# An attention and channel-mixing kernel: weights scaled in plain order and read with a step, some transposes by DMA, tiles in pairs, a new order

## The chip, the cores and the metric

The kernel runs on one core of one Trainium2 chip. The metric is device time in microseconds. Each version is launched several times; one launch is recorded by the hardware profiler, and its "span" runs from the first to the last instruction. The timed figure lies some 2 us above the span (170.61 against 168.7 for the profiled run of the kernel before).

In the profile the engines are PE (TensorE matmuls), PEld (its weight loads, which run beside matmuls), DVE (VectorE), ACT (ScalarE), POOL (GpSimd) and SP (SyncE, which here only issues DMAs).

## The reference

Two parts. First a linear attention with decay: for each of 8 heads of width 48 and each of 4 batches, a 48x48 state runs over 768 steps.

```python
for t in range(S):
    cur = np.einsum('bhd,bhe->bhde', u[None] * kt, vt)
    y[:, :, t] = np.einsum('bhd,bhde->bhe', rt, state + cur)
    state = w[None, :, :, None] * state + np.einsum('bhd,bhe->bhde', kt, vt)
```

Then, on rows of 8 x 48 = 384 channels, a normalization and a channel mix:

```python
xn = (x - mu) / np.sqrt(var + 1e-06) * g_ln
ch = np.maximum(xn @ w_ch1, 0.0) @ w_ch2      # 384 -> 1536 -> 384
return x + ch
```

## The kernel before

The 3072 rows are cut into 24 tiles of 128. For each tile the kernel loads r, k and v, scales r and k by powers of w, turns both (transposes them, so that channels lie on partitions), forms the 128x128 products of r and k for each head, masks them, multiplies by v, adds the state's share, normalizes, turns the normalized row, and runs the two matmul layers: "up" (384 to 1536, with w1) and "down" (1536 to 384, with w2). The last step of a tile is its eviction `ot`, then the store.

Everything is scheduled by hand. One long string, `PLAN`, lists the steps in program order as `name,index,engine` (v is DVE, s is ACT, g is POOL); each engine executes its share of the list in that order. `TR` and `LT` are the turns by PE (of r and k, and of the normalized row), `SW` scales a piece of w1 by minus g, `UP`, `RL` and `DN` are the up matmuls, the relu and the down matmuls, `ST` the statistics, `AM` the mask, `IW2` the load of a third of w2 and `LW1` of a third of w1. `DU` gives PE empty matmuls (on the tile `warm`) while it has nothing else to do.

The parts that matter here:

```python
GROUPS = [1, 1, 1, ...]        # 24 groups of one tile
w1_sb = [[const.tile([P, FB, P], BF16, ...) for kc in range(CK)] for n in range(NW)]   # FB = 4 blocks of 128

def SW(i, e):
    n, kc = divmod(i, CK)
    o, s = w1_sb[n][kc][:].rearrange("p a q -> p q a"), w1_f[n][:, kc].rearrange("p (q a) -> p q a", a=FB)
    g = g_neg[:, kc : kc + 1]
    if e == "s":
        nc.scalar.activation(out=o, in_=s, func=ACT.Copy, scale=g)
    elif e == "v":
        nc.vector.tensor_scalar(out=o, in0=s, scalar1=g, scalar2=None, op0=ALU.mult)
    ...

def UP(i, e):
    ...
            for kc in range(CK):
                nc.tensor.matmul(
                    out=t[:, a * gw : (a + 1) * gw],
                    lhsT=w1_sb[n][kc][:, fb],
                    rhs=xT(g)[:, kc, :gw], ...)
```

`SW` gathers the 512 columns of a piece into four blocks, column 4q + a into block a. After that each block is a contiguous weight for `UP`.

## Time and profile before

| | kernel before |
|---|---|
| time, median of 3 runs | 170.84 us (170.42 to 170.99) |
| span of the profiled run | 168.7 us |
| first tile's eviction starts | 39.5 us |
| eighteenth tile's (tile 17's) eviction starts | 135.7 us |
| last eviction starts | 165.1 us |

The page's busy shares and four of its rows by slice. Each digit is the busy tenth in one fortieth of the span (4.2 us); PEclk is the clock that was granted to PE, in tenths of full speed:

```profile
PE 151.2 (90%) x2185; PEld 121.6 (72%) x2185; DVE 135.7 (80%) x280; ACT 85.7 (51%) x134; POOL 86.4 (51%) x133
PE   7998284398999999999899899999999999999991
ACT  3368999951165544355544256446542644542340
PEclk9999959999999999999999999999999999999999
DMA  5999998802999699959799898971011110110211
```

PE is busy 90% of the span, but slices 5 to 8 show 2, 8, 4 and 3: there it waits, ACT is at 9, and the clock drops once.

### The profile page before, as it was taken

To read this page: it belongs to the slowest core of one execution; us is meant where nothing else is said; L and a number is where in the kernel's file an instruction comes from. 1 tells how busy PE (TensorE), PEld (TensorE's weight loads), DVE (VectorE), ACT (ScalarE), POOL (GpSimd) and SP (SyncE) were. 2 spreads that over 40 slices of the span, in tenths; PEclk is the share of its full clock that TensorE was granted. 3 is DMA by queue.
4 is the path that set the end of the run, shared out by engine and by line. 5 is a ranking of instruction groups with operands and counts; after the bars stand their busy time and mean duration, and the time that the engine had idled before them with its cause. 6 is when DMAs were issued, how large, how long until landed. Compare 5 with 4: busy or idle time off the path is not lost.

```text
span 168.7 us, 5218 instructions
## 1 busy us (share of the span) xinstructions
PE 151.2 (90%) x2185; PEld 121.6 (72%) x2185; DVE 135.7 (80%) x280; ACT 85.7 (51%) x134; POOL 86.4 (51%) x133
## 2 busy tenths in 40 slices
PE   7998284398999999999899899999999999999991
PEld 4978183385677878787688678879786788896770
DVE  3579629078999899999999999999969999787411
ACT  3368999951165544355544256446542644542340
POOL 3547949013296457932671598635532769462200
PEclk9999959999999999999999999999999999999999
DMA  5999998802999699959799898971011110110211
GB/s 87 208 254 279 294 177 158 134 8 57 215 183 202 150 207 196 198 148 207 151 203 229 164 231 175 201 140 51 0 51 47 51 47 4 47 49 4 96 47 47
DMA packets 81225, 22.75 MB, mean 135 GB/s; under 512 B 76593, under 2 KB 79666, under 8 KB 81202
## 3 DMA queue, kind: packets, MB, share of 16 engines
q1 hardware_dynamic: 79938, 21.24, 55.2%
q0 software_dynamic: 432, 1.18, 4.1%
q8 instruction: 17, 0.28, 0.7%
q10 hardware_dynamic: 832, 0.00, 0.3%
q14 instruction: 6, 0.05, 0.1%
HBM read 18.88 MB, written 4.72 MB: 140 GB/s over the span
## 4 chain that ended last, share of the span: by engine, by line
PE 60%; DVE 18%; ACT 13%; DMA 3%; issue 2%; POOL 1%; SPq 0%; DVEq 0%
PE hp L496 21%; PE o L524 20%; ACT w_sb L313 10%; PE tr L345 4%; PE o L261 3%; DVE ot L534 3%; PE at L364 3%; DVE A L374 3%; DMA out_dram<-ot 3%; DVE q L202 2%; PE y L445 2%; PE tr L481 2%; PE y L437 1%; PE s L408 1%; DVE sck L202 1%
## 5 line engine op out<-in xcount | busy, mean ns | idle before, releaser
L496 PE MATMUL hp<-xT,w_sb 128*128 128x128 bf16 x864 | 58.1, 220 | 7.4 <-ACT w_sb L313 3.6
L512 ACT ACTIVATE hT<-hp 128x512 bf16<-128x512 f32 x69 | 42.2, 615 | 44.2 <-PE hp L496 43.0
L496 PEld LDWEIGHTS <-w_sb 128*128 128x128 bf16 x864 | 51.5, 98 | 11.1 <-ACT w_sb L313 5.9
L524 PE MATMUL o<-w_sb,hT 128*128 128x384 bf16 x288 | 56.2, 326 | 1.0 <-DVE ot L534 1.0
L427 POOL TENSOR_TENSOR Vb<-vf,cc 128x384 f32<-128x384 f32 x24 | 22.0, 916 | 29.7 <-DVE cc L199 16.0
L524 PEld LDWEIGHTS <-hT 128*128 128x128 bf16 x288 | 24.9, 97 | 13.8 <-issue 1.3
L374 DVE TENSOR_TENSOR A<-at,mask 128x1024 bf16<-128x1024 f32 (+1 forms) x26 | 29.3, 1128 | 3.1 <-PE at L364 3.0
L534 DVE SCALAR_TENSOR_TENSOR ot<-o,rs,x 128x384 f32<-128x384 f32 x24 | 14.7, 611 | 8.0 <-PE o L524 7.6
L202 POOL TENSOR_TENSOR Z<-ZS,WLZ 128x384 bf16<-128x384 f32 x16 | 17.0, 1065 | 6.9 <-DVE ZS L421 6.8
L313 ACT ACTIVATE w_sb<-w_f,g_neg 128x512 bf16<-128x512 f32 x7 | 18.1, 2660 | 0.0
L473 POOL TENSOR_SCALAR rs<-mv 128x1 f32<-128x1 f32 x24 | 6.9, 287 | 19.2 <-DVE mv L459 18.2
L476 POOL TENSOR_TENSOR rs<-rs,expo 128x1 f32<-128x1 f32 x24 | 14.5, 604 | 2.0
L452 DVE TENSOR_TENSOR x<-y,Vb 128x384 f32<-128x384 f32 x24 | 13.4, 557 | 2.1 <-POOL Vb L427 1.5
L197 ACT COPY xT<-tr 128x384 bf16<-128x384 bf16 x15 | 8.0, 535 | 13.7 <-PE tr L481 13.7
L202 DVE TENSOR_TENSOR sck<-kf,Fk 128x384 bf16<-128x384 f32 x19 | 10.9, 575 | 4.1 <-ACT Fk L278 3.6
L197 ACT COPY trs<-tr 128x1024 bf16<-128x1024 bf16 (+1 forms) x12 | 10.3, 871 | 6.7 <-PE tr L345 6.7
L455 DVE BATCH_NORM_STATS2 stats<-x 128x6 f32<-128x384 f32 x24 | 13.2, 551 | 0.2
L261 PE MATMUL o<-warm 128*128 128x128 bf16 x127 | 11.6, 260 | 1.2 <-DVE warm L225 1.2
L202 DVE TENSOR_TENSOR q<-trs 128x512 bf16<-128x512 bf16 x22 | 10.9, 493 | 1.6 <-ACT trs L197 1.4
L261 PEld LDWEIGHTS <-warm 128*128 128x128 bf16 x127 | 9.9, 120 | 2.4 <-DVE warm L225 1.2
L421 DVE TENSOR_TENSOR ZS<-s,Z 128x384 f32<-128x384 f32 x16 | 8.7, 545 | 3.1 <-ACT cc L197 3.1
L202 DVE TENSOR_TENSOR scr<-rf,Fr 128x384 bf16<-128x384 f32 x19 | 11.1, 583 | 0.1
(65 smaller groups left out, 193.6 us busy)
## 6 DMA issues: line engine op xcount, KB each, us to landing
kf<-in_k_dram SPq DMA_DIRECT2D x24, 192.0 KB, 3.9
rf<-in_r_dram SPq DMA_DIRECT2D x24, 192.0 KB, 3.7
vf<-in_v_dram SPq DMA_DIRECT2D x24, 192.0 KB, 3.7
out_dram<-ot SPq DMA_DIRECT2D x24, 192.0 KB, 2.3
w_f<-in_moe_w_ch_dram SPq DMA_DIRECT2D x3, 768.0 KB, 6.4
w_sb<-in_moe_w_ch_dram POOLq DMA_DIRECT2D x3, 384.0 KB, 6.4
w_p<-in_w_dram ACTq DMA_DIRECT2D x2, 0.8 KB, 2.3
u_p<-in_u_dram ACTq DMA_DIRECT2D x2, 0.8 KB, 3.5
```

The lines of the kernel that those rows point to most:

```text
L197: nc.scalar.copy(out=out, in_=in_)
L202: engines[e].tensor_tensor(out=out, in0=in0, in1=in1, op=ALU.mult)
L261: nc.tensor.matmul(out=warm_ps[0][:, :P], lhsT=warm[:, : P * step : step], rhs=warm[:, :P], start=True, stop=True)
L313: nc.scalar.activation(out=o, in_=s, func=ACT.Copy, scale=g)
L374: nc.vector.tensor_tensor(out=AA(i)[:, a:b].rearrange("p e q t -> p (e q) t"), in0=psum["at", i][:, a:b].rearrange("p e q t -> p (e q) t") ...
L427: nc.gpsimd.tensor_tensor(out=Vb(i)[:].rearrange("p (h d) -> p h d", h=H), in0=vf(i)[:], in1=cc(i)[:].unsqueeze(2).to_broadcast([P, H, D]) ...
L452: nc.vector.tensor_tensor(out=xx(i)[:], in0=psum["y", i][:, :C], in1=Vb(i)[:], op=ALU.add)
L476: nc.gpsimd.tensor_tensor(out=rs[g][:], in0=rs[g][:], in1=expo[:, :n], op=ALU.pow)
L496: nc.tensor.matmul(out=t[:, a * gw : (a + 1) * gw], lhsT=w1_sb[n][kc][:, fb], rhs=xT(g)[:, kc, :gw], start=(kc == 0), stop=(kc == CK - 1),)
L512: nc.scalar.activation(out=o, in_=s, func=ACT.Relu)
L524: nc.tensor.matmul(out=psum["o", i][:, :C], lhsT=hT(g)[:, fk, j * P : (j + 1) * P], rhs=w2_sb[d][:, a, :], start=(fk == 0), stop=(fk == FK ...
L534: nc.vector.scalar_tensor_tensor(out=ot(i)[:], in0=psum["o", i][:, :C], scalar=rs[g][:, j : j + 1], in1=xx(i)[:], op0=ALU.mult, op1=ALU.add,)
```

## The change

Its intent, in the order of the diff:

1. **Plain order.** `SW` scales w1 as it lies; `UP` reads its 128 weights with a step of 4 instead.
2. **Logarithm of the row.** The logarithm of w is taken on one row and broadcast, not broadcast first; powers of w for the state come from an exponential on ACT and no longer from repeated squaring on POOL.
3. **DMA turns.** The keys of tiles 18 to 23 and the normalized rows of tiles 14 to 23 are turned by DMA (`TKD`, `LTD`), not by PE.
4. **Pairs.** Tiles 4 to 21 form nine groups of two: up matmuls of 256 columns, one relu and one set of reciprocal roots for both.
5. **New order.** The whole `PLAN` is new. It loads w1 earlier, moves the small loads of w and u from ACT's queue to SP's, and draws attention work of later tiles forward.

```diff
-GROUPS = [1, 1, 1, 1, 1, 1, 1, 1, 1, 1, 1, 1, 1, 1, 1, 1, 1, 1, 1, 1, 1, 1, 1, 1]
+GROUPS = [1, 1, 1, 1, 2, 2, 2, 2, 2, 2, 2, 2, 2, 1, 1]
+K_BY_DMA = [18, 19, 20, 21, 22, 23]
 PLAN = """
   ... (every line replaced)
-    w1_sb = [[const.tile([P, FB, P], BF16, name=f"w1_sb{n}_{kc}") for kc in range(CK)] for n in range(NW)]
+    w1_sb = [[const.tile([P, FW], BF16, name=f"w1_sb{n}_{kc}") for kc in range(CK)] for n in range(NW)]
   ...
     def ROWS(i, e):
-                nc.scalar.dma_start(
+                nc.sync.dma_start(
   ...
     def WBM(i, e):
-        nc.tensor.matmul(out=t[:, :C], lhsT=ones[:], rhs=w_row[:], start=True, stop=True)
+        nc.tensor.matmul(out=t[:, :C], lhsT=ones[:], rhs=ln_row[:], start=True, stop=True)
   ...
     def SW(i, e):
-        o, s = w1_sb[n][kc][:].rearrange("p a q -> p q a"), w1_f[n][:, kc].rearrange("p (q a) -> p q a", a=FB)
+        o, s = w1_sb[n][kc][:], w1_f[n][:, kc]
   ...
     def TR(i, e):
-        for a, s in enumerate((scr, sck)):
+        for a, s in enumerate((scr,) if i in K_BY_DMA else (scr, sck)):
   ...
+    def LTD(i, e):
+        g, j, _ = group_of[i]
+        nc.sync.dma_start_transpose(out=xT(g)[:, :, j * P : (j + 1) * P], in_=xn(i)[:])
+
+    def TKD(i, e):
+        flat = sck(i)[:].rearrange("p h d -> p (h d)")
+        nc.sync.dma_start_transpose(out=trs(i)[:, 1], in_=flat)
   ...
     def UP(i, e):
-                    lhsT=w1_sb[n][kc][:, fb],
+                    lhsT=w1_sb[n][kc][:, fb::FB],
```

## The prediction

> **What bounds the kernel now.** I read the page first (busy shares, then the span in slices), then a table of stages, then the chain that ended last, then single groups. The stages, with columns length, busy us and count for PE, weight loads, DVE, ACT and POOL, granted clock, DMA share and GB/s:
>
> ```profile
> 0.00:8.00 8.00, 6.76 (x50) 5.50 (x51) 3.23 (x17) 2.89 (x4) 3.28 (x16) 1.00 0.82 146
> 8.00:16.00 8.00, 7.14 (x132) 6.40 (x130) 6.56 (x15) 5.21 (x9) 4.70 (x10) 1.00 0.96 246
> 16.00:24.00 8.00, 4.29 (x62) 3.68 (x63) 4.29 (x7) 8.00 (x7) 5.95 (x8) 0.86 0.99 256
> 24.00:33.00 9.00, 4.45 (x61) 3.59 (x58) 4.44 (x8) 9.00 (x10) 4.89 (x6) 0.93 0.95 168
> ...
> 48.00:83.00 35.00, 33.62 (x493) 26.16 (x490) 33.89 (x64) 18.74 (x36) 20.65 (x29) 1.00 0.87 186
> 83.00:110.00 27.00, 26.33 (x413) 21.67 (x414) 26.38 (x54) 12.74 (x23) 17.98 (x25) 1.00 0.91 193
> 110.00:140.00 30.00, 29.74 (x447) 23.84 (x444) 27.74 (x61) 14.20 (x26) 14.47 (x22) 1.00 0.19 53
> 140.00:165.00 25.00, 25.00 (x352) 19.88 (x346) 16.27 (x33) 10.05 (x18) 9.46 (x15) 1.00 0.12 42
> ```
>
> Four regimes. From 16 to 33 us ACT is busy without a gap and PE half idle, at a clock that once drops. From 48 to 110 DVE is busy 60.3 of 62 us (97%). From 110 to 165 PE is the bound. The last 3.7 us are the last eviction and store. The chain of waits says what ACT does in the first regime:
>
> ```profile
> 13.48 4.87 ACT w_sb L313 x2
> 18.35 0.32 ACT xn L465
> 18.67 2.65 ACT w_sb L313
> 21.32 0.32 ACT xT L197
> 21.63 2.47 ACT w_sb L313
> 24.10 0.42 ACT hT L512
> 24.57 2.47 ACT w_sb L313
> ```
>
> It scales w1 by minus g, seven times, while reordering each row (step 4 on the read side). The groups, with busy us and mean ns:
>
> ```profile
> L313 ACT ACTIVATE w_sb<-w_f,g_neg 128x512 bf16<-128x512 f32 x7 | 18.1, 2660 | 0.0
> L197 ACT CAST vv<-vf 128x384 bf16<-128x384 f32 x10 | 5.1, 513 | 4.7 <-PE s L408 2.3 <-DMA vf<-in_v_dram 1.8 <-PE y L445 0.6
> L374 DVE TENSOR_TENSOR A<-at,mask 128x1024 bf16<-128x1024 f32 (+1 forms) x26 | 29.3, 1128 | 3.1 <-PE at L364 3.0
> ```
>
> A plain cast of 384 columns takes ACT 513 ns; 512 reordered columns take 2660. PE's first dense stretch begins only at 33.2 us, and the first tile's last down matmul ends at 39.5 (its eviction starts then).
>
> **What the skill says.** "TensorE: Matmul & The Clock Gate", Weight-path perf modes, lets the fast weight load read its four chunks of 32 columns "packed or strided". The kernel before has a probe: the last 6 of its first 14 warm-up loads have step 4. They show 152 ns, as the unit-step ones do, and the same 107 ns pace, but on the cold clock; warm, where N=128 matmuls go at 56 ns, no run here shows it. "SBUF — State Buffer", Who interferes with whom: GpSimd and a vector instruction in a two-port mode, or with two SBUF inputs, lock each other out. The trace agrees: the same DVE cast of v takes 343 ns at least and 1174 at most. "VectorE: DVE Perf Modes", The three transpose paths, gives 1309 ns for a 128x128 DMA transpose; no row of this trace has one. "DMA: Bandwidth & Descriptors", Issuing engines are not separate DMA queues: moving the w and u rows to SP gains no bandwidth, they join the others' engines; at the start these show 0.96 to 0.99 busy, which agrees.
>
> **Part 1, w1 in plain order.** ACT scales six pieces instead of seven, each an estimated 0.62 us (513 ns x 512/384 is 0.68; the 128x512 relu has 615 ns): 18.1 falls to 3.7 us. POOL's 2.7 us piece goes, DVE has three of about 0.45 us for one of 1.49. On the path this is about 17.4 us of chain (L313, 10.3% of 168.7), but not all is won, as DMA comes next. In the new SP order the third w1 piece stands behind 9 tile loads and two other pieces: 1.77 + 2.36 = 4.1 MB, and half a w2 piece (0.2) beside it. The trace before had moved 3.5 MB at 16.9 us and 4.7 at 21.1 (sum of the slices), so it lands at about 20 us. The w2 pieces are issued on POOL only after uwI, which now needs the u and w rows behind the first w1 piece (2.4 MB, about 13 us), so they start at 14 to 18 us and land by about 25 (6.4 us each before, sharing). The logarithm on one row changes no length: log, broadcast matmul (1.64 us), exp in a new order, w_row arriving at 2.8 us as before. Tile 0's own chain, by the old durations in the new order on DVE and ACT: transposes 8.8, mask done 14, cc 15.5, x 17, xn 18.6, xT 19.4. So up matmuls run from 19.5, and from there I count on PE's queue 6.3 us of work up to tile 0's last down matmul: **26 us instead of 39.5, 13 us earlier**. But PE had also done more by then before: 14.0 us of useful work against 9.4 now. Net gain of the start: 13.5 - 4.6, about **9 us**.
>
> **Part 2, PE's work.** With the spacings of the chain (12 up matmuls 0.67 us, 4 down 0.65, 8 transposes 0.45): 24 key transposes and 30 of xn go to DMA, 54 x 56 ns = 3.0 us; 324 matmuls of 256 columns instead of 648 of 128 save some 2.4 ns per pair, 0.8 us. **3.8 us less**, of 131.7 in all. The DMA transposes are late (tiles 14 and 18 on), when DMA is 0.19 busy, with some 5 us of other PE work between issue and need.
>
> **Part 3, DVE.** Gone or smaller: 9 copies of 128x1024 (0.64 each) become 9 half ones (0.37), while ACT takes 3 more whole ones, 3 relus, 3 xT, 2 r scalings; new: 5 casts of v, 2 q, 1 xn. In all about -1.5 us of 135. What counts is where: up to which point. I summed the DVE instructions in program order between the last down matmul of tile 0 and that of tile 17, at the start-to-start times they have between 48 and 110 us (mask 1.14, bn_stats 0.50, ot 0.54, scalings 0.52 and 0.54, x 0.48, q 0.44, cast 0.62, xn 0.55, copy 0.64). Before: 184 instructions, **92.9 us**, against 88.4 of PE; the trace took 95.8 (39.5 to 135.3), so the sum explains it within 3%. After: 212 instructions, **106.8 us**, against 96.8 of PE. The new order pulls four tiles more of attention into that stretch (20 masks instead of 16), leaving 1 mask after it instead of 4.
>
> **The sum.** Tile 0 at 26. Then DVE-bound: 106.8, and I take 104 to 110, since POOL loses 9 pairs of rs instructions and some products (about 86 to 71 us busy), which eases the lock, while in-order waits cost the 3% seen. Tile 17 at about 133. Then PE: 127.9 - 106.2 = 21.7, plus 2% (before 29.7 for 29.3): 155. Tail 3.7: span about 159. The timed figure is 2.1 us above the profiled span: **161 us**, rounded down to 160.5 for the chance that the lock eases more.
>
> **Rivals.**
> 1. *DVE is no bound, PE is.* Then from 26 us follow 118.5 of PE with the 1 to 2% loss of the last stretch before: 146.5, tail 3.7, offset 2.1: 152 to 154 us. For: DVE's two-port casts go at half these times when POOL is idle. Against: DVE's 97% in 48 to 110 us, and more front-loading now.
> 2. *DMA holds the start.* It is 0.95 to 0.99 busy from 8 to 33 us. If the w2 pieces or tile 3's loads land 4 us later, all shifts: 164 to 165.
> 3. *The strided weight load costs when warm.* In the 6 one-tile groups 216 matmuls at 56 ns have no room: at twice the time 12 us, part of it beside DVE-bound work: 166 to 170. With 256 columns (109 ns by the spacing) it would hide; that the groups became pairs speaks for some fear of this. The probe at 152 ns against 152 speaks against.
> 4. *DMA transposes late.* 16 of them wait in SP's order behind stores; each that comes late stops PE directly, in the PE-bound part. At 1 us each outside the cover: 10 us at worst, 2 likely at most.
>
> **Range and chances.** Start 9 us (5 to 12), PE's 3.8 us won in the tail part, 2 to 4 given back where DVE has more to do earlier: net 10. The range 155.5 to 165.5 goes from the lock easing with half of rival 1 to rival 2 or a mild rival 3. Faster by 2% means below 167.4: 0.93; within: 0.06; slower: 0.01, since only rivals 3 and 4 together would do it.
>
> **What would show it.** L313-like rows of ACT at about 0.6 us; first eviction at 26 us (24 to 29), else part 1 is wrong; DVE 95% busy or more from 30 to 130 us with PE at 90%, else part 3; weight loads of w1 at about 98 ns and up matmuls of 128 columns still 56 ns apart; DMA transposes landing within 3 us; PE solid after 133. If DVE has gaps in the middle while PE is solid, rival 1 holds; if both idle on transposes, rival 4.

## The result, and the profile after

| | before | after |
|---|---|---|
| time, median of 4 runs | 170.92 us (170.42 to 172.91) | 163.34 us (162.81 to 164.15) |
| ratio | 1 | 0.954 (95%: 0.9454 to 0.9626) |
| span of the profiled run | 168.7 | 162.4 |
| first eviction starts | 39.5 | 29.6 |
| from there to tile 17's | 96.2 | 105.7 |
| from there to the last | 29.4 | 23.4 |
| from there to the end | 3.6 | 3.6 |

A ratio here is the mean time of one kernel's runs over the mean of the other's runs in the same rounds, so it is not quite the ratio of the medians quoted beside it. Executions over 1.5% slower than the fastest of the same kernel are left out of the means.

The change is 4.6% faster. The page after, the rows that answer to those shown of before (one slice is 4.1 us):

```profile
PE 148.9 (92%) x1823; PEld 120.2 (74%) x1823; DVE 131.5 (81%) x282; ACT 72.4 (45%) x129; POOL 73.1 (45%) x102
PE   7998699989999999999999899899899799999690
ACT  4203753438586853646566123353146152442220
PEclk9999969999999999999999999999999999999998
DMA  4999997989999994994889998552322423120311
```

The hole of PE in slices 5 to 8 has closed except for one slice with a 6, and ACT's nines are gone. PE's number of instructions fell from 2185 to 1823, its busy time by only 2.3 us. What appeared are smaller dips late in the row (7, 6) where before there was a nearly unbroken line of nines.

The stages, with the columns of the prediction's table (length; busy us and count for PE, weight loads, DVE, ACT, POOL; clock; DMA share, which can read a little above 1; GB/s):

```profile
16.00:24.00 8.00, 6.09 (x96) 5.46 (x94) 5.70 (x11) 4.99 (x11) 4.25 (x7) 0.83 1.11 270
24.00:33.00 9.00, 8.98 (x117) 7.09 (x117) 7.42 (x17) 3.50 (x6) 5.60 (x8) 0.96 0.93 182
...
48.00:83.00 35.00, 34.13 (x444) 28.05 (x443) 34.85 (x71) 20.32 (x37) 23.18 (x28) 1.00 0.86 185
83.00:110.00 27.00, 25.92 (x302) 20.68 (x300) 26.42 (x60) 11.39 (x20) 13.80 (x15) 1.00 0.80 182
110.00:130.00 20.00, 18.29 (x227) 14.15 (x224) 18.91 (x40) 6.85 (x13) 8.61 (x11) 1.00 0.30 71
130.00:158.00 28.00, 26.69 (x279) 21.05 (x277) 13.53 (x29) 10.64 (x18) 6.44 (x10) 1.00 0.21 67
```

From 16 to 33 us PE now has 15.1 us of work where it had 8.7, and ACT 8.5 of 17 where it had no gap. The DMA share stays high (1.11 and 0.93 here). In the middle DVE is at 99%; in the last 28 us PE is at 95% where it had been solid.

The chain that ended last, from 11 to 30 us (start, length, what; here and in the chains below, `issue` pieces of under 0.05 us are left out):

```profile
11.05 7.16 DMA w_f<-in_moe_w_ch_dram
18.23 1.33 ACT w_sb L305 x2
19.57 0.40 ACT vv L197
19.97 0.62 ACT w_sb L305
20.59 0.51 ACT xn L457
...
21.15 0.47 PE tr L481 x3
...
22.60 3.04 PE hp L496 x36
25.66 0.82 PE o L524 x4
...
29.60 0.62 DVE ot L534
```

Where seven scalings of some 2.5 us stood, there are now three of 0.62 to 0.67 us behind a DMA: a third of w1, issued at 11.05 us, lands at 18.2. ACT works in the order of `PLAN`, so tile 0's normalized row `xn` waits behind these scalings, and its turn and the up matmuls behind `xn`. The 36 up matmuls take 3.04 us, half as long again as 36 x 56 ns = 2.0: part of them ran while the clock was down (0.83 in that row).

The groups, with busy us and mean ns of one:

```profile
L305 ACT ACTIVATE w_sb<-w_f,g_neg 128x512 bf16<-128x512 f32 x6 | 4.2, 719 | 5.0 <-DMA w_f<-in_moe_w_ch_dram 5.0
L496 PE MATMUL hp<-xT,w_sb 128*128 128x256 bf16 (+1 forms) x540 | 57.0, 255 | 3.2 <-DMA xT<-xn 2.7
L496 PEld LDWEIGHTS <-w_sb 128*128 128x128 bf16 x540 | 48.3, 115 | 6.8 <-DMA xT<-xn 3.2
L366 DVE TENSOR_TENSOR A<-at,mask 128x1024 bf16<-128x1024 f32 (+1 forms) x26 | 29.4, 1129 | 1.3 <-PE at L356 1.3
```

One scaling on ACT takes 719 ns instead of 2660. The weight load with a step takes 115 ns in the mean instead of 98. Up matmuls waited 2.7 us for turned rows (`xT<-xn` by DMA), a wait that was not there before.

**A ledger.** To compare versions with different orders, I split the span in four. *Work* is PE's useful work by the spacings that the prediction used: 131.7 us before, 127.9 after. *Lost at the start* is the start of the first eviction less the PE work placed before it (14.0 us in the old order, 9.4 in the new). *Lost later* is what PE lost between first and last eviction, the *tail* is the rest. The rows below come from the profiled runs:

| run | span | first eviction | work | lost at start | lost later | tail |
|---|---|---|---|---|---|---|
| before | 168.7 | 39.5 | 131.7 | 25.5 | 7.9 | 3.6 |
| after | 162.4 | 29.6 | 127.9 | 20.2 | 10.7 | 3.6 |
| after, run again with the experiments | 160.4 | 28.4 | 127.9 | 19.0 | 9.9 | 3.6 |

So of 25.5 us lost at the start only 5 to 6.5 were won back, the work fell by 3.8, and 2 to 3 were lost anew later. (Between the two profiled runs of the changed kernel lies 2.0 us: the first has the dip of the clock, the second has none. Over the four timed runs of the first set the two at clock 1.0 average 162.95 and the two at 0.986 and 0.988 average 163.9.)

### The profile page after: what moved, and what is told of

Read it like the earlier page. It is cut to its first block, busy times and chain, and to the rows that moved or that the text cites.

```text
span 162.4 us, 4487 instructions
## 1 busy us (share of the span) xinstructions
PE 148.9 (92%) x1823; PEld 120.2 (74%) x1823; DVE 131.5 (81%) x282; ACT 72.4 (45%) x129; POOL 73.1 (45%) x102
## 3 DMA queue, kind: packets, MB, share of 16 engines
q0 software_dynamic: 432, 1.18, 3.7%
## 4 chain that ended last, share of the span: by engine, by line
PE 40%; DVE 34%; DMA 11%; SPq 6%; issue 4%; ACT 2%; POOL 1%; DVEq 0%; POOLq 0%
PE hp L496 18%; PE o L524 15%; DMA xT<-xn 6%; DVE A L366 6%; DMA w_f<-in_moe_w_ch_dram 4%; DVE q L202 4%; DVE ot L534 4%; DVE sck L202 3%; DVE x L444 3%; DVE stats L447 3%; DVE ZS L413 3%; DVE xn L459 2%; DVE scr L202 2%; PE at L356 2%; SPq L315 1%
## 5 line engine op out<-in xcount | busy, mean ns | idle before, releaser
L496 PE MATMUL hp<-xT,w_sb 128*128 128x256 bf16 (+1 forms) x540 | 57.0, 255 | 3.2 <-DMA xT<-xn 2.7
L496 PEld LDWEIGHTS <-w_sb 128*128 128x128 bf16 x540 | 48.3, 115 | 6.8 <-DMA xT<-xn 3.2
L419 POOL TENSOR_TENSOR Vb<-vf,cc 128x384 f32<-128x384 f32 x24 | 22.7, 947 | 19.2 <-DVE cc L199 14.0
L366 DVE TENSOR_TENSOR A<-at,mask 128x1024 bf16<-128x1024 f32 (+1 forms) x26 | 29.4, 1129 | 1.3 <-PE at L356 1.3
L202 DVE TENSOR_TENSOR sck<-kf,Fk 128x384 bf16<-128x384 f32 x19 | 13.1, 693 | 4.0 <-ACT Fk L274 4.0
L260 PE MATMUL o<-warm 128*128 128x128 bf16 x143 | 13.2, 267 | 1.0 <-DVE warm L225 1.0
L465 POOL TENSOR_SCALAR rs<-mv 128x2 f32<-128x2 f32 (+1 forms) x15 | 3.9, 259 | 22.3 <-DVE mv L451 22.1
L260 PEld LDWEIGHTS <-warm 128*128 128x128 bf16 x143 | 11.6, 123 | 2.5 <-issue 1.3
L447 DVE BATCH_NORM_STATS2 stats<-x 128x6 f32<-128x384 f32 x24 | 13.3, 553 | 0.2
L468 POOL TENSOR_TENSOR rs<-rs,expo 128x2 f32<-128x2 f32 (+1 forms) x15 | 10.5, 697 | 1.2
L202 POOL TENSOR_TENSOR scr<-rf,Fr 128x384 bf16<-128x384 f32 x7 | 8.1, 1169 | 5.7 <-DMA rf<-in_r_dram 4.8
L356 PE MATMUL at<-trs 48*128 48x128 bf16 x192 | 9.7, 222 | 0.4 <-DMA trs<-sck 0.4
L337 PE MATMUL tr<-ident,scr 128*128 128x128 bf16 x96 | 9.5, 223 | 0.3 <-ACT xT L197 0.2
```

Source lines behind the costliest of these rows:

```text
L202: engines[e].tensor_tensor(out=out, in0=in0, in1=in1, op=ALU.mult)
L260: nc.tensor.matmul(out=warm_ps[0][:, :P], lhsT=warm[:], rhs=warm[:], start=True, stop=True)
L356: nc.tensor.matmul(out=t[:, par, q, :], lhsT=trs(i)[p0 : p0 + D, 1, q, :], rhs=trs(i)[p0 : p0 + D, 0, q, :], start=True, stop=True,)
L366: nc.vector.tensor_tensor(out=AA(i)[:, a:b].rearrange("p e q t -> p (e q) t"), in0=psum["at", i][:, a:b].rearrange("p e q t -> p (e q) t") ...
L419: nc.gpsimd.tensor_tensor(out=Vb(i)[:].rearrange("p (h d) -> p h d", h=H), in0=vf(i)[:], in1=cc(i)[:].unsqueeze(2).to_broadcast([P, H, D]) ...
L447: nc.vector.bn_stats(out=stats[i % 4][:], in_=xx(i)[:])
```

## The experiments

Twelve kernels ran in three sets, each set on one chip beside the kernel before, whose median was 170.81, 170.71 and 170.59 us. The theory going in was that the plain order gives nearly all of the gain. The rivals were that the new order and the DMA turns give a good part, that the stepped weight load costs something and the pairs exist to hide it, and for the middle that DVE, PE, or both set the pace.

### First set: parts alone

**Plain order alone.** The kernel before with nothing but these three lines:

```diff
-    w1_sb = [[const.tile([P, FB, P], BF16, ...
+    w1_sb = [[const.tile([P, FW], BF16, ...
-        o, s = w1_sb[n][kc][:].rearrange("p a q -> p q a"), w1_f[n][:, kc].rearrange("p (q a) -> p q a", a=FB)
+        o, s = w1_sb[n][kc][:], w1_f[n][:, kc]
-                    lhsT=w1_sb[n][kc][:, fb],
+                    lhsT=w1_sb[n][kc][:, fb::FB],
```

> The kernel before with one part of the change alone: w1 scaled in plain order, weights read with step 4; its groups of one tile, its order and its logarithm stay. Theory (scaling on ScalarE held the start): scaling instructions fall from 2660 to about 720 ns, the first eviction comes at 29 to 33 us instead of 39.5, and 6 to 9 us are won: 162 to 165 us, so most of the whole change. Rival (the stepped weight load costs when the clock is warm, which is why the pairs came): all 864 up matmuls have 128 columns here, at twice 56 ns they cost 48 us more, at 70 ns 12 us more; time 171 or above. Rival (the new order made the gain): 169 to 171.

Correct, 162.26 us (161.21 to 163.7, that last run slow), ratio 0.9484 (0.9411 to 0.9556). That is the gain of the whole change. Its stages:

```profile
16.00:24.00 8.00, 6.41 (x106) 5.29 (x106) 7.83 (x17) 6.31 (x12) 7.39 (x13) 1.00 1.15 278
24.00:33.00 9.00, 8.29 (x128) 6.93 (x126) 6.66 (x13) 3.52 (x7) 2.76 (x4) 1.00 0.79 160
```

PE is busy 14.7 of 17 us and the clock stays at 1.00. Up matmuls begin at 18.4 us, the first eviction at 31.1 with 14.0 us of work done by then: 17.1 lost at the start, 8.4 less than before, and 7.9 lost later, as before.

**All the rest.** The changed kernel with those three lines undone:

```diff
-        o, s = w1_sb[n][kc][:], w1_f[n][:, kc]
+        o, s = w1_sb[n][kc][:].rearrange("p a q -> p q a"), w1_f[n][:, kc].rearrange("p (q a) -> p q a", a=FB)
   ... (tile and weight as in the kernel before)
```

> The kernel after with that one part undone: scaling reorders again, weights are read densely. Theory: six ScalarE pieces at 2.1 us instead of 0.66 from issue to issue put 6 to 9 us on the start, first eviction at 36 to 38 us instead of 29.6, time 169 to 172. Rival (DMA holds the start, the scaling would hide behind the arrival of w1): at most 2 us more, 163 to 165.5.

Correct, 172.4 us (171.34 to 173.49, 20 runs), ratio 1.0118 (1.0087 to 1.0148). The four other parts together, on the old scaling, are 1.2% slower than the kernel before. One row shows how:

```profile
24.00:33.00 9.00, 5.88 (x62) 4.96 (x62) 3.20 (x6) 7.32 (x9) 2.53 (x4) 0.50 0.93 182
```

PE waits for ACT, falls to half its clock for the whole stretch, and the first eviction starts at 37.8 us. The new order has 4.6 us less PE work to offer while the scalings last (14.0 less 9.4). That may be why it loses more there (28.4 us in the ledger below, against 25.5 before); no run tested it.

**Turns by TensorE.** The changed kernel, all DMA turns given back to PE, the copies out of PSUM to ACT:

```diff
-K_BY_DMA = [18, 19, 20, 21, 22, 23]
+K_BY_DMA = []
-CC,16,v DN,46,- SK,19,v RL,133,s Q,17,v LTD,14,- VB,16,g UP,131,- ...
+CC,16,v DN,46,- SK,19,v RL,133,s Q,17,v LT,14,- XT,14,s VB,16,g UP,131,- ...
   ... (LTD,i becomes LT,i and XT,i,s; TKD,i becomes TCk,i,s)
```

> The kernel after with the 16 DMA transposes undone: TensorE turns the late rows and keys (54 more transposes of 56 ns = 3.0 us), ScalarE copies them out. Theory: the DMA turns won 3.0 us of TensorE and gave 2.7 us back in three waits for their landing, so about nothing: 162.5 to 164.5. Rival (prediction part 2: they win their full 3 us): 165.5 to 167. Rival (they lose): 160 to 162.

Correct, 166.53 us (165.69 to 167.5), ratio 0.9765 (0.9684 to 0.9847), against 0.954 and 0.9511 for the changed kernel in its two sets: 2.4 to 2.7% slower, about 4 us. My expectation of almost no difference fell; the full 3.0 us of 54 transposes is real within this order, and some more with it. The ledger has 3.0 us more work and nearly the same losses (19.2 at the start, 10.6 later): PE's waits for DMA are gone, but waits for the ACT copies take their place.

**Pairs as 128 columns.** The changed kernel, each up matmul of 256 columns made into two of 128, each with its own stepped load:

```diff
-                nc.tensor.matmul(
-                    out=t[:, a * gw : (a + 1) * gw],
-                    lhsT=w1_sb[n][kc][:, fb::FB],
-                    rhs=xT(g)[:, kc, :gw], ...
+                for j in range(size):
+                    nc.tensor.matmul(
+                        out=t[:, a * gw + j * P : a * gw + (j + 1) * P],
+                        lhsT=w1_sb[n][kc][:, fb::FB],
+                        rhs=xT(g)[:, kc, j * P : (j + 1) * P], ...
```

> The kernel after with its order and its groups, but each 256-column up matmul split into two of 128 columns, each with its own stepped weight load (324 loads and matmuls more). Theory: 113 ns of load overlap at a pace of 56 ns, so only 324 x about 2.5 ns = 0.8 us: 163.5 to 165. Rival (the pairs are needed to hide the stepped load): at a pace of 70 ns 9 us more, at 113 ns 37 us more, 172 to 200.

Correct, 161.07 us (160.62 to 161.74), ratio 0.9438 (0.9378 to 0.9497): not the 163.5 to 165 expected; if anything faster than the pairs, though the intervals overlap. The loads (min, median, max in ns) and the matmuls:

```profile
L497 PEld LDWEIGHTS <-w_sb x864: 110/113/134, 20.6 to 152.9; 128*128 128x128 bf16 x173
L497 PE MATMUL hp<-xT,w_sb x864: 216/219/248, 20.8 to 153.0; 128*128 128x128 bf16 x173
```

A stepped load takes 113 ns where a plain one took 98, but each matmul is as long as before (219 ns here, 219 median before) and follows the last at the same 56 ns: loads run ahead, beside the matmuls. The rival of a costly stepped load falls, and with it the reason that I had imagined for the pairs.

### Second set: what holds the middle

Here the changed kernel ran again as a base:

> The kernel after, unchanged, on the same chip and in the same rounds as the next ones, since a4 came 2.3 us below the after of another job. Theory (the 1.7 us by which a4's start was ahead came from the moment at which the cold clock fell in that profiled run, and from arrival of w1, not from the split): this reads 160.5 to 164 with a spread between runs. Rival (the pairs themselves cost 2 us): 162.8 to 164.2 in every run.

Correct, 162.18 us (161.4 to 163.11), ratio 0.9511 (0.9437 to 0.9585). Its first eviction starts at 28.4 us, tile 17's 105.6 us later. The chain at its start, in a run without the dip of the clock:

```profile
10.01 4.98 DMA u_p<-in_u_dram
...
15.16 0.21 POOL uwI L202
...
17.45 7.75 DMA w_sb<-in_moe_w_ch_dram
25.25 0.81 PE o L524 x4
```

It leads through the small row u (landed at 15.0) to POOL's product uwI, and from there to a third of w2, which POOL issues afterwards and which lands at 25.2. That is the second third. Four lines of PE's timeline (others between them left out; in brackets the idle time before and what ended it) show who needs what:

```profile
15.69 0.24 PE L387 MATMUL s<-uwI,q 128*128 128x2 bf16 x4 [1.36 <-POOL uwI L202]
20.98 2.35 PE L496 MATMUL hp<-xT,w_sb 128*128 128x128 bf16 x36
23.16 0.82 PE L524 MATMUL o<-w_sb,hT 128*128 128x384 bf16 x4
25.25 0.81 PE L524 MATMUL o<-w_sb,hT 128*128 128x384 bf16 x4 [1.05 <-DMA w_sb<-in_moe_w_ch_dram]
```

Tile 0's attention itself waits for uwI (1.36 us). The up matmuls begin at 21.0, the first four down matmuls at 23.2; only the next four wait for w2, 1.05 us.

**A quarter of the statistics.** Wrong on purpose (relative error 0.20): DVE's statistics read 96 columns, not 384.

```diff
-        nc.vector.bn_stats(out=stats[i % 4][:], in_=xx(i)[:])
+        nc.vector.bn_stats(out=stats[i % 4][:], in_=xx(i)[:, :96])
```

> The kernel after, but bn_stats reads 96 columns of 384 (wrong result on purpose): about 0.3 us less VectorE work per tile, 20 tiles between the first and the 18th eviction. Theory (that stretch is bound by VectorE, 105.8 us measured of 106.8 summed): 5 to 6 us less there, 157 to 159 in all. Rival (TensorE bounds it, VectorE is merely busy): within 1 us of the kernel after.

160.7 us (159.77 to 161.97), ratio 0.9427 (0.9346 to 0.9509): 1.5 us less than the base (the intervals overlap, so the size is rough), where a pure DVE bound asks for over 5 (nearly 20 statistics in the stretch to tile 17, 0.3 us saved on each). The statistics fell from 550 to 249 ns, the stretch to tile 17 only from 105.6 to 104.4.

```profile
48.00:83.00 35.00, 34.91 (x461) 29.43 (x459) 34.46 (x73) 21.36 (x38) 21.34 (x26) 1.00 0.88 188
```

DVE is still busy 98%, because other instructions of it grew: in 33 to 110 us the casts of v went from 434 to 589 ns in the mean and the scalings of k from 692 to 763 (the q products fell, from 561 to 514), with POOL hardly less busy. And PE is at 34.9 of 35: it has nothing left to give there.

**Fewer down matmuls.** Wrong on purpose (relative error 0.39): 3 of 12 down matmuls left out in tiles 1 to 14, 42 x 163 ns = 6.8 us of PE work.

```diff
         for a in range(n):
+            if a == 1 and 1 <= i <= 14:
+                continue
```

> The kernel after, but 9 instead of 12 down matmuls for tiles 1 to 14 (wrong result on purpose): 14 x 3 x 162 ns = 6.8 us less TensorE work in the middle. Theory (VectorE-bound): 0 to 2 us less. Rival (TensorE-bound): 5 to 7 us less.

159.08 us (158.44 to 159.39), ratio 0.9322 (0.9258 to 0.9386): 3.1 us less than the base, of 6.8 removed; the stretch to tile 17 fell from 105.6 to 103.0.

```profile
48.00:83.00 35.00, 32.98 (x434) 27.31 (x433) 34.84 (x72) 21.55 (x38) 21.97 (x26) 1.00 0.88 189
```

PE now has gaps (33.0 of 35) and DVE has none. So neither engine alone sets the middle. Roughly, by one cut of each, relief for DVE is worth a quarter of itself and relief for PE somewhat under half: from 33 to 110 us the base has DVE busy 99% and PE 96%.

**Turns in the old order.** Plain order alone, with key turns (tiles 18 to 23) and row turns (tiles 15 to 21) by DMA:

```diff
+K_BY_DMA = [18, 19, 20, 21, 22, 23]
-        for a, s in enumerate((scr, sck)):
+        for a, s in enumerate((scr,) if i in K_BY_DMA else (scr, sck)):
   ... (LTD and TKD as in the changed kernel; LT,i and XT,i of tiles 15 to 21 become LTD,i; TC,i becomes TCr,i and TKD,i)
```

> Kernel a1 (old order, plain order of w1) plus the DMA turns of the keys of tiles 18 to 23 and of the normalised rows of tiles 15 to 21. Theory: its last stretch (tile 17 to 23, 29.8 us) and a part before are bound by TensorE, so 45 transposes x 56 ns = 2.5 us less, minus waits for landings: 159 to 161, below both kernels. Rival (late DMA turns land too late in an order not made for them): 162 to 165.

Correct, 161.6 us (161.43 to 161.98), ratio 0.9482 (0.9407 to 0.9558): no better than plain order alone (0.9484) and above the 159 to 161 expected, though PE has 2.5 us less work. PE's longest wait after 95 us (total us, times, longest):

```profile
PE hp L505 <- DMA xT<-xn: 2.6, 3, 1.1
```

The turned rows come late: normalized row to up matmul is a short path, and the DMA puts over 2 us into it. The 2.6 us of waits are as much as the 2.5 us of work saved.

### Third set: the start, and a better version

**Small rows early.** The changed kernel with the rows of w and u issued from ACT right after the logarithm, so that uwI, and with it w2, need not wait:

```diff
-MW,0,v WF,0,- ... LK,1,- LN,0,s DU,4,- WBM,0,-
+MW,0,v WF,0,- ... LK,1,- LN,0,s ROWS,0,- DU,4,-
-                nc.sync.dma_start(
+                nc.scalar.dma_start(
```

> The kernel after, but the rows of w and u are fetched early from ScalarE's queue, right after the logarithm, as the kernel before did (not behind the first w1 piece on SP). The chain of waits of the kernel after runs through u_p, uwI, the issue of w2 and its landing at 25.2 us. Theory (that late fetch is what put my 26 us off): uwI at about 8 us instead of 15.2, w2 issued earlier, first eviction at 25.5 to 27 instead of 28.4, time 159.5 to 161. Rival (bandwidth holds the start: the same 5.3 MB have to come first): first eviction at 27.5 to 29, time 161.5 to 163.

Correct, 164.83 us (164.43 to 165.07), ratio 0.9651 (0.9602 to 0.97): slower than the changed kernel run again (its interval ends at 0.9585), while the interval of its first set overlaps a little; and above both ranges expected. The loads of w1, from issue to landing, and the chain:

```profile
DMA to landing us min/median/max: 8.3/9.7/11.3
```

```profile
8.23 8.34 DMA w_f<-in_moe_w_ch_dram
...
23.46 2.91 PE hp L496 x36
```

In the base the three thirds of w1 took 6.1 us in the median; here the first third of w2 starts beside them at 8.0 us and they take 9.7. Scaling begins at 16.6 instead of 13.7, up matmuls at 23.3 instead of 21.0, at a low clock again (0.86 from 16 to 24 us), and the first eviction at 30.3. Only that first third came early: POOL, which works in order too, waits for tile 0's `cc` and issues the other two at 19.4, against 17.5 in the base. So the run shows that one transfer moved forward pushed others back; it is no clean test of all of w2 issued early. A sum fits a start held by the amount of data: the base's stages add up to 5.4 MB moved by 24 us, and nine tile loads (1.77 MB), w1 (2.36) and w2 as written (1.18) come to 5.3.

**The same, pairs split as above.**

> c1 with the 256-column up matmuls split into two of 128 columns (as a4). In the same job as c1: theory (the split itself costs about 0.8 us, a4's lead was the draw of another job): 0 to 1.5 us more than c1. Rival (the pairs cost, smaller matmuls let TensorE start on a half group or keep the clock up): 1 to 2 us less than c1.

Correct, 163.84 us (163.29 to 164.86), ratio 0.9585 (0.9527 to 0.9643). The edit is that of the fourth kernel, on the one above. About 1 us less than with pairs in the same rounds, where 0 to 1.5 us more was expected (the intervals overlap). PE's waits for turned rows are 0.6 us in both split versions, and 2.7, 1.6 and 2.1 us in the three profiles with pairs. Why splitting shortens them I did not settle.

**Old order with key turns only.** Plain order alone, plus the key turns of the six last tiles by DMA, no row turns:

```diff
+K_BY_DMA = [18, 19, 20, 21, 22, 23]
-        for a, s in enumerate((scr, sck)):
+        for a, s in enumerate((scr,) if i in K_BY_DMA else (scr, sck)):
+    def TKD(i, e):
+        flat = sck(i)[:].rearrange("p h d -> p (h d)")
+        nc.sync.dma_start_transpose(out=trs(i)[:, 1], in_=flat)
   ... (in PLAN: TKD,i after SK,i, TCr,i for TC,i, for tiles 18 to 23)
```

> a1 (old order, plain order of w1) plus only the DMA turns of the keys of tiles 18 to 23; the normalised rows stay on TensorE, since in b3 three waits for those cost 2.6 us. Theory: 24 x 56 ns = 1.3 us less TensorE work and no wait: 160 to 161.5, below a1 (162.3) and b3 (161.6). Rival (key turns wait too): 162 or more.

Correct, 160.31 us (159.21 to 160.63), ratio 0.9377 (0.9321 to 0.9434): the lowest of all correct versions, just below the changed kernel in both of its sets (its intervals begin at 0.9437 and 0.9454) and not clear of the first set's split pairs (0.9438). Its waits of PE after 95 us, all of them:

```profile
PE hp L506 <- DVE xT L201: 0.2, 1, 0.2
PE tr L491 <- DVE xn L469: 0.2, 1, 0.2
```

A key is turned long before it is used, so the DMA's delay is hidden; 24 transposes (1.3 us) leave PE for nothing. Against plain order alone (0.9484, from another set) the interval overlaps slightly, so the 1% between these two is likely, not certain. Of the 2.8 us between their profiled spans 1.3 are the work and 1.4 arose before the first eviction, where both run the same list; that part is the spread between runs.

**The same with w2 issued earlier.**

```diff
-TCk,1,s AMa,0,v LG,0,- CC,0,s LW1,0,- TCr,1,s ZU,0,v VB,0,g DU,9,- Y,0,- ...
+TCk,1,s AMa,0,v LG,0,- CC,0,s LW1,0,- TCr,1,s ZU,0,v VB,0,g IW2,0,g DU,9,- Y,0,- ...
   ... (IW2,1 after VB,1 and IW2,2 after ZD,1)
```

> c3 with the three w2 pieces issued earlier on GpSimd (after the first, second and second-last of its first products, so at about 12.5, 14 and 15.5 us instead of 15.7, 21.4 and 24.3). TensorE waited 1.0 us for a w2 piece in a1. Theory (the start is held by DMA bandwidth): within 1 us of c3. Rival (held by the issue of w2): 1 to 2.5 us less than c3, best of all, 158.5 to 160.

Correct; four runs of 161.87, 166.0, 167.08 and 165.86 us, the last three over 1.5% above the first. No ratio follows from one fast run. But that fast run's profile tells what happened: its first eviction starts at 32.9 us, not 29.7, and its chain has

```profile
13.75 13.28 DMA rf<-in_r_dram
```

A load of r for one tile, usually 3.8 us, took 13.3 beside the weights. Pulling one transfer forward pushes another back.

The ledger of the kernels that settle the question:

| run | span | first eviction | work | lost at start | lost later | tail |
|---|---|---|---|---|---|---|
| plain order alone | 160.2 | 31.1 | 131.7 | 17.1 | 7.9 | 3.6 |
| all the rest | 169.6 | 37.8 | 127.9 | 28.4 | 9.7 | 3.6 |
| turns by TensorE | 164.3 | 28.6 | 130.9 | 19.2 | 10.6 | 3.6 |
| after, again | 160.4 | 28.4 | 127.9 | 19.0 | 9.9 | 3.6 |
| old order, key turns | 157.4 | 29.7 | 130.4 | 15.7 | 7.9 | 3.4 |

How far can a row from one profile be trusted? Up to the first eviction the three correct kernels of the old order in plain order run the same list (leaving out the one with w2 issued earlier), and lost 17.1, 15.9 and 15.7 us there. Four profiles share the new order's start: the changed kernel twice, turns by TensorE and split pairs lost 20.2, 19.0, 19.2 and 18.4. So differences under some 2 us at the start are within the spread, but the new order's start is the costlier one in every pair of them.

## Why the prediction was right or wrong

**Right: the verdict and the size.** 163.34 us lies in the range, 2.8 above the point. By its own sum, 26 + 106.8 + 22.1 + 3.7 made 159 of span; the profiled run made 29.6 + 105.7 + 23.4 + 3.6 = 162.3. Nearly all of the miss is in the first term.

**The start: the mechanism was right, one term was mis-sized.** The scalings did fall to 719 ns (0.62 us predicted; their pace, 0.66, is closer), and DMA did come next. The step that failed is tile 0's own chain, "so up matmuls run from 19.5". They began at 22.4 us in the profiled run and at 21.0 in the second profile. The chain was summed from durations on DVE and ACT and left two DMA arrivals out. First, the row u was dated "about 13 us" and put only on the way to w2; it landed at 15.0 (second profile), and tile 0's own matmuls need its product uwI: `cc` was done at 16.3 and 16.4 in the two profiles where 15.5 was counted. Second, in the profiled run, ACT waited 1.05 us for a third of w1 (landed at 18.2) and then scaled before it came to tile 0's `xn`, which started at 20.5 although its statistics were ready at 19.6. This late start is 2.9 of the 3.6 us by which the eviction (29.6) missed 26, and 1.5 of 2.4 in the second profile (28.4).

The rest is the step after it, "6.3 us of work" on PE's queue: it took 7.2 us in the profiled run, where the 36 up matmuls needed 3.0 instead of 2.0 at the lower clock, and 7.4 in the second, where a w2 piece, dated right ("by about 25", 25.2), held PE for 1.05 us. The prediction had set 24 to 29 as its own test; the two profiles fall on either side of it. Its second rival, DMA holding the start, was the better account, in a milder form. The cure tried in the third set, small rows issued early, made the kernel slower (0.9651 against 0.954 and 0.9511), so their late issue is not the whole cause.

**The net gain of 9 us at the start was 5 to 6.5.** Plain order in the old order won 8.4. The new order reaches its first eviction 2.7 us sooner than that (28.4 against 31.1) but with 4.6 us less done.

**PE's 3.8 us: right, and given back.** The work is gone; with the turns returned to PE the kernel is about 4 us slower. But the new order as a whole (its second profile) lost 1.9 us more at the start than plain order alone and 2.0 us more later, which adds up to 3.9. The first figure is no larger than the spread of single profiles, though all of them point the same way. This is where the expected gain went: four of the five parts, worth 3.8 us on paper, net nothing that these runs can tell from zero. The prediction's fourth rival, late DMA turns, is part of it (1.6 and 2.7 us of waits, "2 likely at most").

**The middle: the number was right, the reason half right.** 106.8 was predicted from DVE's sum and 105.7 came. But PE's own sum, 96.8, stretched by the ratio that the kernel before showed (95.8 over 88.4) gives 104.9, so the match proves nothing, and the two cuts show that neither engine is the bound alone: 1.5 us won of over 5 taken from DVE, 3.1 of 6.8 taken from PE. The prediction's own test asked for PE at 90% there; it was at 95 to 96%. "DVE-bound" should have been "both within 4% of full, and each waits for the other now and then". The first rival (PE alone, 152 to 154) fell too.

**The stepped weight load: right that it costs nothing.** It showed 113 ns, not "about 98", but the pace stayed at 56 ns. One slip of wording: the prediction puts the jumps of the old scaling "on the read side"; by the code the read is in order and the write jumps. No number rested on it.

**The last stretch: 23.4 us (22.8 in the second profile) for 22.1.** The prediction had asked for PE solid after tile 17; it was 95% busy. The largest wait there was for a DMA turn, that of tile 23's row, which took 3.8 us to land where "within 3 us" was expected.

**What stays open:** why the up matmuls of split pairs wait less for turned rows, and how the 2 us of further loss in the middle divide between the front-loaded attention and the pairs; no run took the new order apart. Nor did any run change the logarithm alone; it is one of the four parts that together gain nothing clear of noise. How early all of w2 can be issued without delaying w1 is open too.

## What to carry to other kernels

When a change has many parts, run its likeliest part alone and everything else without it: here three lines out of a whole rewrite gave as much as all of it, and a simpler kernel built on them came out at or below the rewrite. Before summing a chain from the durations of its engines, list every input that it needs, also what arrives by DMA and what stands ahead of it in an engine's order, and put each date on the path. What moving work to DMA is worth depended on the order around it: in the old order keys turned early cost PE no wait, while rows turned just before their use cost in waits what they saved; in the new order giving all turns back to PE cost about 4 us.

## What the Trainium skill lacked or had wrong

- **The cost of a scattered write.** "SBUF — State Buffer", Door 1: The DMA port swizzle, says that SBUF has lines of 16 bytes and that each access to a new line pays, with no figure for ScalarE or VectorE. Here 128x512 elements written 256 bytes apart took ACT 2660 ns and DVE 1493, in plain order 719 and 480 (median). The direction agrees; here the factor is 3.1 on DVE and 3.7 on ACT.
- **The cost of a stepped weight load.** "TensorE: Matmul & The Clock Gate", Weight-path perf modes, allows columns "packed or strided" without a time. Step 4 in bf16 took 113 ns instead of 98, and matmuls of 128 columns kept their 56 ns. So the step cost no time here, which fits the page.
- **DMA transposes.** "VectorE: DVE Perf Modes", The three transpose paths, gives 1309 ns for 128x128. Here one DMA turned three or four such blocks and landed in 2.4 us in the median (up to 3.8), so they took less than that multiple of the page's figure. No page that I read gives the time of SP's issue, 1.19 us for a transpose, against 0.53 in the median for a plain store here.
- **Locks between DVE and POOL.** "SBUF — State Buffer", Who interferes with whom, describes the lock, but not how much of a relief is spent again: with the statistics cut from 550 to 249 ns, casts of v grew from 434 to 589 ns and only some 1.5 of over 5 us was won. That the lock did it was not tested.
- **Issuing from more engines.** "DMA: Bandwidth & Descriptors", Issuing engines are not separate DMA queues, agrees: with a third of w2 issued earlier from POOL, the w1 thirds issued from SP landed in 9.7 us instead of 6.1.
